# Attention inside a feed-forward kernel: plain heads' q and k change engines, steps of batches one to four change slots

## The chip, the core and the metric

The kernel runs on one core of a Trainium2 chip. The core has five engines with an instruction queue each: TensorE (PE, the matmuls), ScalarE (ACT), VectorE (DVE), GpSimd (POOL, which here issues the loads) and SyncE (SP, which here issues the stores and the DMA transposes). They run beside each other and wait for one another by semaphores. The metric is the device time of one execution in microseconds (us), the median of several runs.

## The reference

q, k and v have 8 batches, 8 heads, 576 tokens and 64 values a head. Heads 0 to 3 ("plain") let a token look at itself and the 31 tokens before it; heads 4 to 7 ("dilated") at every fourth token back to 128:

```python
mask_plain = (rel >= 0) & (rel < window)                                      # window = 32
mask_dil = (rel >= 0) & (rel < window * dilation) & (rel % dilation == 0)     # dilation = 4
scores = np.where(masks[None, :, :, :], scale * (q @ k^T), -1000000000.0)
attn = softmax(scores);  o = attn @ v
x = o.transpose(0, 2, 1, 3).reshape(8 * 576, 512)
h = np.maximum(x @ w_in, 0.0);  out = (h * h) @ w_out                         # w_in 512x2048, w_out 2048x512
```

(The two lines with `@` and `softmax` are shortened from the reference.) The 4608 rows of x go through the feed-forward layer (FFN) with a squared relu; the output is float32.

## The kernel before

**Storage.** On the chip everything is bf16, sums are float32 in PSUM. Heads go in pairs `e`: 0 and 1 are plain, 2 and 3 dilated. x is kept transposed in the ring `xT` (features on partitions, four batches of tokens), which the attention writes and the FFN reads.

**FFN.** Tokens go in four tiles of 256 and then tiles of 512. A tile is a list of *groups*: first-layer groups (`g1`, `mm1`, L660 to L682) are four matmuls of 512 columns (or eight of 256) into a bank of the pool `ps_f`, a relu on ACT into `h2T` (L681) and its square on DVE (L682). Second-layer groups (`g2`, L697 to L712) are four matmuls into another bank of `ps_f`; after the fourth of them ACT copies the bank to `osb` (L711) and SP stores it (L634). The last 128 tokens are done in two column halves of 256. In the kernel before both halves live in one bank. 512 tokens make 32 groups, all of them 288.

**Attention.** It is cut into steps, named by the batch, a letter and the head pair:

- `L` loads q and k (`q`) or v by POOL; `L..:x` is the DMA transpose of q and k on SP (`cross`, L213)
- `q`, `k`, `Q`, `K` (capitals: second part of the tokens): q or k is transposed and copied to `qT` or `kbd`. In batch 1, and for batch 2's plain heads, PE transposes into a bank of `ps_a` and the copies read PSUM (`trans`, L221 to L238); in the other cases the copies read what the DMA transposed (`xx`). Four copies to a step for the plain heads and for q (`halves`, L240 to L267)
- `v`, `V`: a dilated head's v is spread into `vbd` (two DVE copies, L207)
- `a`, `b`: scores of the first and second part: matmuls of `kbd` and `qT` into `ps_a`, an Exp on ACT, a mask product on DVE (L295 to L317)
- `o`, `p`: matmuls by v into `po` and sums into `pd` (L413, L415), Ln and Exp of the sums on ACT (L417, L418), and their product on DVE into `xT` (L428) (`pv`)

**Banks.** PSUM has `ps_f` with four banks, `ps_a` with two, and one each for `po` and `pd` (L111 to L114). A step that takes a bank waits until the bank's last reader is done. The odd pairs of batch 1 take two of `ps_f` for `po` and `pd` (L450 and L451).

**Which engine copies.** For plain heads q goes by ACT in batches 1 to 3 and by DVE from batch 4 (`ADDED = 4`), k always by DVE; dilated heads copy both on DVE (L225, L440).

**Order.** The order of all instructions is that of the program: the scheduler is manual, and each engine's queue follows it. The main loop (L836 to L848) emits one FFN group and after it the attention steps that the string `PROGRAM` (L21 to L36) has between its bars for this place. I call a group with the steps behind it a *slot*: slot n is group n (counted from 0 in the order in which the groups run) and then what stands behind bar n + 1. From batch 5 on most steps come from a formula with fixed offsets (L826 to L832), which isn't touched. The first field of `PROGRAM` is batch 0's attention in finer steps, run before any group.

Of the kernel before, what the change touches and what calls it, by code (L numbers as in the profile page):

```python
# [23 lines left out]
    "T20k C20v T30 C30v h W3 S20 E20 W2 S30 E30 T01 C01v T11 C11v W2 P00 P10 D00 D10 L00 X00 M00 B01 B11 P20 "  # L24
    "P30 D20 D30 L20 X20 M20 S01 T21 C21a T31 C31v E01 W2+11 S11 E11 | B21 S21 E21 | B31 S31 E31 P21 P31 D21 "
    "D31 L21 X21 M21 L31 X31 M31 | | P01 P11 D01 D11 L01 X01 M01 L11 X11 M11 | | | | | | | | | | | | | m n | | "
    "| | | L2:q00123 L2:q10123 | 1q1 1q3 | 1q2 1k2 | 1k1 1v3 | 1a2 | 1v2 1k0 1q0 | 1o2 | 1a0 1a1 | 1k3 1o0 1o1 "
    "| 1a3 1Q0 | 1K0 1o3 | 1Q1 1K1 | 1Q2 | 1b0 | | 1Q3 1K2 L2:vwpdr L3:q00123 L3:q10123 | L2:x | | 2q0 | | 2k0 "
    "1V2 | 1b2 1p0 | 1b1 1V3 1K3 | | 1p2 1p1 | 2a0 1b3 | 2k1 2o0 2b0 1p3 | 2q1 2k2 L3:x | | 2q2 2p0 L3:vwpdr "
    "2a1 | | | 2b1 | 2o1 2q3 2a2 | | 2p1 2v2 | 2k3 | 2b2 2o2 | 2v3 | 2a3 2p2 L4:q10123 | 2b3 3k1 | 2o3 3q1 | | "  # L30
    "3a1 L4:q00123 2p3 | 3k0 3k2 | | 3o1 | | | 3q0 3v2 | | | | 3a0 | 3b1 3k3 | | | 3p1 L4:x 3q2 L4:vwpdr | | "
    "3b0 | 3a2 3q3 3o0 4k0 | | | 3o2 3b2 | | 3p0 3v3 | 4q1 3a3 | 3p2 4q2 4q0 | L5:q10123 3b3 | 3o3 | 4k1 | | "
    "L5:q00123 3p3 4k2 4k3 4a0 L5:vwpdr | | | 4b0 | | 4q3 | | 4o0 | | | 4a2 4v2 | 4b2 | 4a3 L5:x 4a1 | 4o2 | | "
    "| 4p2 L6:q00123 4v3 | | 4b1 | | 4p0 | | 4p1 | 5q0 5k0 | 4b3 | | | | 4o1 | | 5k2 L6:q10123 4o3 | 5q2 5k1 | "
    "| 4p3 | 5q1 |"
)  # L36


# [25 lines left out]
def kernel(  # L64
# [9 lines left out]
    nc = tc.nc  # L74
    P = nc.NUM_PARTITIONS
    B, H, S, D = q.shape
    DM, DFF = moe_w_in.shape
    NTOK = B * S
# [7 lines left out]
    NE = H // 2  # L86
# [9 lines left out]
    PARTED = (0, 1)  # L96
    STAGE = (0, 1, 0, 2, 2, 2, 0, 1)
    ADDED = 4
# [51 lines left out]
    def staged(b: int, nm: str):  # L150


        t = rb[STAGE[b]][nm]
        return t[:, :].rearrange("p (a h x) -> p a h x", h=H, a=2)
# [47 lines left out]
    def spread_v(b: int, e: int, parts):  # L202

        p0, p1 = parts[0], parts[-1] + 1
        for hl in range(2):
            rows = slice(64 * hl, 64 * hl + 64)
            nc.vector.tensor_copy(  # L207
                vbd[b % 2][rows, e, RES * p0 : RES * p1, rows],
                vds[b][rows, e - NE // 2, p0:p1, :].rearrange("p m (r d) -> p (m r) d", d=D),
            )  # L210
# [7 lines left out]
            staged(b, nm)[0:n, part, h0:, :].rearrange("p h x -> p (h x)"),  # L218
        )

    def trans(b: int, e: int, nm: str, part: int):  # L221

        ps = ps_a.tile([P, 1024], bf16, name="pa")
        t = staged(b, nm)
        copy = nc.scalar.copy if nm == "q" and e < NE // 2 else nc.vector.tensor_copy  # L225
        if b == 2:
            m0, n, pitch, cuts = 0, M, M, [(t[0:80, a, :, :], MS[a], 80) for a in range(2)]
        else:

            m0, n, pitch, cuts = MS[part], MN[part], 80, [(t[0:80, part, :, :], 0, 80)]  # L230
        pv_ = ps[:, 0 : 4 * pitch].rearrange("p (h c m) -> p h c m", h=2, c=2)
        for hl in range(2):
            for c in range(2):
                for src, c0, w in cuts:
                    nc.tensor.transpose(  # L235
                        pv_[:, hl, c, c0 : c0 + w], src[:, 2 * e + hl, P * c : P * c + P], ident[0:w, 0:w]
                    )
        halves(e, nm, pv_[:, :, :, 0:n], m0, n, copy)  # L238
# [193 lines left out]
    def step(b: int, code: str):  # L432

        what, e = code[0], int(code[1])
        part = int(what in "QKVbp")
        if what in "qk" and (b > XB or b == XB and e >= NE // 2):
            t = (qx if what == "q" else kx)[b % 2]
            by_act = what == "q" and e < NE // 2 and b < ADDED  # L440
            halves(
                e, what, t[:, 2 * e : 2 * e + 2, :, :], 0, M, nc.scalar.copy if by_act else nc.vector.tensor_copy
            )
        elif what in "qQkK":
            trans(b, e, what.lower(), part)
        elif what in "vV":
            spread_v(b, e, [part] if b in PARTED else [0, 1])
        elif what in "ab":
            scores(b, e, part)
        elif b in PARTED and e % 2:  # L450
            pv(b, e, part, ps_f, "pf")  # L451
        else:
            pv(b, e, part)
# [180 lines left out]
    def store(osb, pos: int, c0: int = 0, c1: int = DM):  # L634

        x = 0
        while x < P:
            b, y = divmod(pos + x, S)
            part = int(y >= RES * MN[0]) if b in PARTED else 0
            w = MN[part] if b in PARTED else M  # L640
            r, m = divmod(y - RES * MS[part], w)
            n = min(P - x, w - m)
            row = b * S + RES * (MS[part] + m) + r
            nc.sync.dma_start(out[row : row + RES * (n - 1) + 1 : RES, c0:c1], osb[x : x + n, c0:c1])
            x += n

    def ffn_groups(tk0: int, nt: int):

        early = NT <= tk0 <= 2 * NT
        h2 = h2_pool.tile([P, NF, NT], bf16, name="h2T")
        per = NT // nt
        kts = (0, 2, 1, 3) if tk0 >= NT else (0, 1, 2, 3) if tk0 == 0 else (2, 3, 0, 1)
        cut = 3 if tk0 >= NT else 2
        cur, acc = {}, {}

        cuts = [(0, nt)] if tk0 // RING == (tk0 + nt - 1) // RING else [(0, -tk0 % RING), (-tk0 % RING, nt)]

        def mm1(u, ks):  # L660
            if u not in acc:
                acc[u] = ps_f.tile([P, NT], f32, name="pf")
            for x in range(per):
                f = per * u + x
                piece = max(y for y in range(len(w_in_sb)) if w_cuts[y] <= P * f)
                c0 = 512 * (f // 4) + f % 4 - w_cuts[piece]
                for kt in ks:
                    for y0, y1 in cuts:
                        t0 = (tk0 + y0) % RING
                        nc.tensor.matmul(  # L670
                            acc[u][:, nt * x + y0 : nt * x + y1],
                            w_in_sb[piece][:, kt, c0 : c0 + 509 : 4],
                            xT[:, kt, t0 : t0 + y1 - y0],
                            start=(kt == kts[0] and x == 0 and y0 == 0),
                            stop=(kt == kts[-1] and x == per - 1 and y1 == nt),
                            skip_group_check=True,
                        )
            if ks[-1] != kts[-1]:
                return
            hv = h2[:, per * u : per * u + per, 0:nt]  # L680
            nc.scalar.activation(hv, acc[u][:, :].rearrange("p (x n) -> p x n", x=per), ACT.Relu)  # L681
            nc.vector.tensor_tensor(out=hv, in0=hv, in1=hv, op=ALU.mult)  # L682

        def g1(i):
            if i < 2 and tk0 < NT:
                for u in range(2):
                    mm1(u, kts[2 * i : 2 * i + 2])
            elif i < 2 and early:
                for u in (2 * i, 2 * i + 1):
                    mm1(u, kts[:cut])  # L690
            elif i < 4 and early:
                for u in (2 * i - 4, 2 * i - 3):
                    mm1(u, kts[cut:])
            else:
                mm1(i, kts)

        def g2(m, part):  # L697
            if part == 0:
                cur[m] = ps_f.tile([P, DM], f32, name="pf")

            last = tk0 + P * (m + 1) == NTOK
            c0, c1 = (DM // 2 * (part // 2), DM // 2 * (part // 2 + 1)) if last else (0, DM)
            f0, f1 = (NF // 2 * (part % 2), NF // 2 * (part % 2 + 1)) if last else (4 * part, 4 * part + 4)
            for f in range(f0, f1):
                nc.tensor.matmul(  # L705
                    cur[m][:, c0:c1], h2[:, f, P * m : P * m + P], w_out_sb[:, f, c0:c1],
                    start=(f == 0), stop=(f == NF - 1),
                )
            if f1 == NF:
                osb = osb_pool.tile([P, DM], f32, name="osb")  # L710
                nc.scalar.copy(osb[:, c0:c1], cur[m][:, c0:c1])  # L711
                store(osb, tk0 + P * m, c0, c1)  # L712

        return [lambda i=i: g1(i) for i in range(NF // per)] + [
            lambda m=m, part=part: g2(m, part) for m in range(nt // P) for part in range(4)
        ]

# [161 lines left out]
```

## Time and profile before

| | |
|---|---|
| median of 6 runs | 314.06 us (312.62 to 315.2) |
| the profiled execution | 314.74 us, span from first to last instruction 313.0 us |
| granted TensorE clock | 0.993 |
| PE busy | 301.9 us, 96% |
| ACT busy | 197.5 us, 63%, 421 instructions |
| DVE busy | 195.6 us, 63%, 633 instructions |
| POOL busy | 94.0 us, 30% |
| DMA | 35.04 MB |

"Busy" is the time in which an engine has an instruction under way, as a share of the span. In the groups and in the timeline a row names the engine, the line of the kernel, the operation, `out<-in` by the program's names with partitions x elements, and how many instructions it counts. A bracket or the last column is the engine's idle time just before, and what ended it. Times in the timeline are from the span's start.

### The profile page before, as it was taken

To read this page: it belongs to the slowest core of one execution; us is meant where nothing else is said; L and a number is where in the kernel's file an instruction comes from. 1 tells how busy PE (TensorE), PEld (TensorE's weight loads), DVE (VectorE), ACT (ScalarE), POOL (GpSimd) and SP (SyncE) were. 2 spreads that over 40 slices of the span, in tenths; PEclk is the share of its full clock that TensorE was granted. 3 is DMA by queue.
4 is the path that set the end of the run, shared out by engine and by line. 5 is a ranking of instruction groups with operands and counts; after the bars stand their busy time and mean duration, and the time that the engine had idled before them with its cause. 6 is when DMAs were issued, how large, how long until landed. Compare 5 with 4: busy or idle time off the path is not lost.

```text
span 313.0 us, 6759 instructions
## 1 busy us (share of the span) xinstructions
PE 301.9 (96%) x2537; PEld 187.6 (60%) x2569; DVE 195.6 (63%) x633; ACT 197.5 (63%) x421; POOL 94.0 (30%) x138
## 2 busy tenths in 40 slices
PE   8899999999999999999999999999999999999994
PEld 3689745968755555565499655555555555445543
DVE  1336568898987878985799469946994334104400
ACT  7278838769878956785378547864686456226511
POOL 8679787626083127401451041000000000000000
PEclk9799999999999999999999999999999999999999
DMA  7999999999989899994699975602200210121022
GB/s 107 195 175 215 202 161 182 195 163 198 140 120 210 118 183 137 141 191 63 89 137 121 167 120 88 115 8 63 67 3 0 69 68 0 36 67 34 2 67 67
DMA packets 79808, 35.04 MB, mean 112 GB/s; under 512 B 49824, under 2 KB 74784, under 8 KB 79776
## 3 DMA queue, kind: packets, MB, share of 16 engines
q0 software_dynamic: 46592, 18.23, 51.6%
q1 hardware_dynamic: 32496, 16.06, 26.1%
q10 hardware_dynamic: 688, 0.33, 0.5%
q8 instruction: 20, 0.33, 0.5%
q14 instruction: 12, 0.10, 0.1%
HBM read 36.90 MB, written 9.44 MB: 148 GB/s over the span
## 4 chain that ended last, share of the span: by engine, by line
PE 84%; ACT 6%; DVE 2%; DMA 2%; issue 2%; POOL 1%; ACTq 0%; POOLq 0%
PE pf L670 37%; PE pf L705 36%; PE po L413 3%; PE pd L415 2%; DMA kb<-in_k_dram 2%; PE pa L304 2%; ACT h2T L681 2%; PE pa L310 1%; ACT qT L248 1%; PE pa L235 1%; ACT rec L417 1%; DVE kbd L252 1%; ACT rec L418 1%; ACT osb L711 1%; DVE xT L428 1%
## 5 line engine op out<-in xcount | busy, mean ns | idle before, releaser
L670 PE MATMUL pf<-xT,w_in 128*128 128x256 bf16 (+1 forms) x758 | 132.6, 325 | 1.1 <-DVE xT L428 0.3
L705 PE MATMUL pf<-w_out_sb,h2T 128*128 128x512 bf16 (+1 forms) x570 | 130.9, 373 | 1.7 <-ACT osb L711 0.5
L670 PEld LDWEIGHTS <-w_in 128*128 128x128 bf16 x768 | 82.3, 114 | 35.9 <-issue 1.2
L681 ACT ACTIVATE h2T<-pf 128x512 bf16<-128x512 f32 x144 | 83.7, 597 | 23.2 <-PE pf L670 22.5
L705 PEld LDWEIGHTS <-h2T 128*128 128x128 bf16 x592 | 54.3, 98 | 54.0 <-issue 0.7
L682 DVE TENSOR_TENSOR h2T<-h2T 128x512 bf16<-128x512 bf16 x144 | 58.0, 423 | 40.0 <-ACT h2T L681 38.4
L711 ACT COPY osb<-pf 128x512 f32<-128x512 f32 (+1 forms) x37 | 21.2, 573 | 42.2 <-PE pf L705 39.9
L428 DVE TENSOR_TENSOR xT<-po,rec 128x288 bf16<-128x288 f32 (+2 forms) x52 | 23.7, 456 | 31.1 <-ACT rec L418 30.4
L178 POOL DMA_DIRECT2D vbd<-in_v_dram x36 | 25.7, 730 | 55.5 <-PE pd L415 49.5
L417 ACT ACTIVATE rec<-pd 128x288 f32<-128x288 f32 (+2 forms) x52 | 21.5, 413 | 24.0 <-PE pd L415 22.9
L314 ACT ACTIVATE pt<-pa 128x352 bf16<-128x352 f32 (+6 forms) x56 | 27.6, 499 | 9.0 <-PE pa L310 4.7
L418 ACT ACTIVATE rec<-rec 128x288 f32<-128x288 f32 (+2 forms) x56 | 24.8, 444 | 1.8
L413 PEld LDWEIGHTS <-vbd 128*128 128x128 bf16 x286 | 16.8, 97 | 10.5 <-DVE vbd L207 1.2
L248 DVE COPY qT<-xx 64x288 bf16<-64x288 bf16 x80 | 20.0, 250 | 1.1
L161 POOL DMA_DIRECT2D qb<-in_q_dram x18 | 13.0, 722 | 22.2 <-DMA xx<-qb 20.8
L252 DVE COPY kbd<-xx 64x288 bf16<-64x288 bf16 x40 | 18.8, 470 | 0.6
L413 PE MATMUL po<-pt,vbd 128*128 128x96 bf16 (+3 forms) x263 | 18.0, 198 | 0.7 <-DVE vbd L207 0.5
L191 POOL DMA_DIRECT2D vd<-in_v_dram x24 | 14.7, 636 | 5.9 <-DMA kb<-in_k_dram 3.1
L415 PE MATMUL pd<-pt,mk 128*128 128x96 bf16 (+5 forms) x158 | 16.3, 203 | 0.0
L161 POOL DMA_DIRECT2D kb<-in_k_dram x18 | 12.8, 713 | 0.8 <-issue 0.8
L304 PE MATMUL pa<-qT,kbd 128*128 128x96 bf16 (+2 forms) x146 | 12.2, 201 | 0.5 <-ACT qT L248 0.5
L197 POOL DMA_DIRECT2D vbd<-in_v_dram x16 | 9.7, 615 | 9.2 <-PE pd L415 7.4
(89 smaller groups left out, 237.0 us busy)
## 6 DMA issues: line engine op xcount, KB each, us to landing
out_dram<-osb SPq DMA_DIRECT2D x18, 128.0 KB, 4.8
qb<-in_q_dram POOLq DMA_DIRECT2D x7, 320.0 KB, 7.5
kb<-in_k_dram POOLq DMA_DIRECT2D x7, 320.0 KB, 9.3
vd<-in_v_dram POOLq DMA_DIRECT2D x32, 64.0 KB, 4.8
w_in<-in_moe_w_in_dram POOLq DMA_DIRECT2D x4, 512.0 KB, 7.5
w_out_sb<-in_moe_w_out_dram POOLq DMA_DIRECT2D x4, 512.0 KB, 12.0
qb<-in_q_dram POOLq DMA_DIRECT2D x7, 256.0 KB, 5.9
kb<-in_k_dram POOLq DMA_DIRECT2D x7, 256.0 KB, 7.4
```

Of the source, the lines that this page charges most:

```text
L161: nc.gpsimd.dma_start(t[0:n, part, hs, :], src[b, hs, t0 : t0 + RES * n, :].rearrange("h (p r) d -> p h (r d)", r=RES))
L178: nc.gpsimd.dma_start(dst[rows, e, i0:i1, rows], v[b, 2 * e + hl, 64 * i0 : 64 * i1, :].rearrange("(i p) d -> p i d", p=64),)
L314: nc.scalar.activation(pt[:, off : off + n], ps[:, 0:n], ACT.Exp, scale=SCALE)
L413: nc.tensor.matmul(oo, vb[:, e, i, :], rh, start=(x == 0), stop=(x == len(mms) - 1), skip_group_check=True)
L417: nc.scalar.activation(rec[:, 0:n], d[:, 0:n], ACT.Ln)
L418: nc.scalar.activation(rec[:, 0:n], rec[:, 0:n], ACT.Exp, scale=-1.0)
L428: nc.vector.tensor_tensor(out=tok, in0=o if o is o3 else o[:, 0:n], in1=rec if o is o3 else rec[:, 0:n], op=ALU.mult)
L670: nc.tensor.matmul(acc[u][:, nt * x + y0 : nt * x + y1], w_in_sb[piece][:, kt, c0 : c0 + 509 : 4], xT[:, kt, t0 : t0 + y1 - y0], start=(kt ...
L681: nc.scalar.activation(hv, acc[u][:, :].rearrange("p (x n) -> p x n", x=per), ACT.Relu)
L682: nc.vector.tensor_tensor(out=hv, in0=hv, in1=hv, op=ALU.mult)
L705: nc.tensor.matmul(cur[m][:, c0:c1], h2[:, f, P * m : P * m + P], w_out_sb[:, f, c0:c1], start=(f == 0), stop=(f == NF - 1),)
L711: nc.scalar.copy(osb[:, c0:c1], cur[m][:, c0:c1])
```

## The change

It has four parts.

1. *Who copies.* A plain head's k is copied by ACT (batches 1 to 4), its q by DVE. A step whose code ends with `a` is copied by ACT whatever it is: `1q1a`, `1Q3a` and `2q3a`.
2. *Banks.* A step whose code ends with `f` takes `po` and `pd` from `ps_f`: `1o1f`, `1p1f`, `1p3f`, `2p1f`, `2p2f`. Before, it was `1o1`, `1o3`, `1p1`, `1p3`.
3. *The last tile* takes a second bank of `ps_f` for its second column half.
4. *Slots.* These differ (loads that stand beside unmoved steps are left out):

| slot | before | after |
|---|---|---|
| 21 | (loads of batch 2) | `1q1a 1q3`, then these loads |
| 22 | `1q1 1q3` | `1q2` |
| 23 | `1q2 1k2` | `1k2 1k1` |
| 24 | `1k1 1v3` | `1v3` |
| 40, 41 | –, `2k0 1V2` | `2k0`, `1V2` |
| 47 | `2k1 2o0 2b0 1p3` | `2o0 1p3f 2b0 2k1` |
| 54, 55, 56 | `2o1 2q3 2a2`, –, `2p1 2v2` | `2o1 2a2 2q3a`, `2v2`, `2p1f` |
| 61, 62, 63 | `2b3 3k1`, `2o3 3q1`, – | `2b3 2o3`, –, `2p3` |
| 64, 65 | `3a1` (a load) `2p3`, `3k0 3k2` | `3k1 3q1` (the load), – |
| 66, 67 | –, `3o1` | `3a1`, `3k0` |
| 68, 69 | –, – | `3o1`, `3k2` |

The other slots hold the same steps (with the suffixes above). In all ACT gets 440 instructions in place of 420, DVE 613 in place of 633; PE has the same number, and POOL and SP the same order.

```diff
--- before.py
+++ after.py
@@ -24,15 +24,15 @@
     "T20k C20v T30 C30v h W3 S20 E20 W2 S30 E30 T01 C01v T11 C11v W2 P00 P10 D00 D10 L00 X00 M00 B01 B11 P20 "
     "P30 D20 D30 L20 X20 M20 S01 T21 C21a T31 C31v E01 W2+11 S11 E11 | B21 S21 E21 | B31 S31 E31 P21 P31 D21 "
     "D31 L21 X21 M21 L31 X31 M31 | | P01 P11 D01 D11 L01 X01 M01 L11 X11 M11 | | | | | | | | | | | | | m n | | "
-    "| | | L2:q00123 L2:q10123 | 1q1 1q3 | 1q2 1k2 | 1k1 1v3 | 1a2 | 1v2 1k0 1q0 | 1o2 | 1a0 1a1 | 1k3 1o0 1o1 "
-    "| 1a3 1Q0 | 1K0 1o3 | 1Q1 1K1 | 1Q2 | 1b0 | | 1Q3 1K2 L2:vwpdr L3:q00123 L3:q10123 | L2:x | | 2q0 | | 2k0 "
-    "1V2 | 1b2 1p0 | 1b1 1V3 1K3 | | 1p2 1p1 | 2a0 1b3 | 2k1 2o0 2b0 1p3 | 2q1 2k2 L3:x | | 2q2 2p0 L3:vwpdr "
-    "2a1 | | | 2b1 | 2o1 2q3 2a2 | | 2p1 2v2 | 2k3 | 2b2 2o2 | 2v3 | 2a3 2p2 L4:q10123 | 2b3 3k1 | 2o3 3q1 | | "
-    "3a1 L4:q00123 2p3 | 3k0 3k2 | | 3o1 | | | 3q0 3v2 | | | | 3a0 | 3b1 3k3 | | | 3p1 L4:x 3q2 L4:vwpdr | | "
-    "3b0 | 3a2 3q3 3o0 4k0 | | | 3o2 3b2 | | 3p0 3v3 | 4q1 3a3 | 3p2 4q2 4q0 | L5:q10123 3b3 | 3o3 | 4k1 | | "
-    "L5:q00123 3p3 4k2 4k3 4a0 L5:vwpdr | | | 4b0 | | 4q3 | | 4o0 | | | 4a2 4v2 | 4b2 | 4a3 L5:x 4a1 | 4o2 | | "
-    "| 4p2 L6:q00123 4v3 | | 4b1 | | 4p0 | | 4p1 | 5q0 5k0 | 4b3 | | | | 4o1 | | 5k2 L6:q10123 4o3 | 5q2 5k1 | "
-    "| 4p3 | 5q1 |"
+    "| | | 1q1a 1q3 L2:q00123 L2:q10123 | 1q2 | 1k2 1k1 | 1v3 | 1a2 | 1v2 1k0 1q0 | 1o2 | 1a0 1a1 | 1k3 1o0 "
+    "1o1f | 1a3 1Q0 | 1K0 1o3 | 1Q1 1K1 | 1Q2 | 1b0 | | 1Q3a 1K2 L2:vwpdr L3:q00123 L3:q10123 | L2:x | | 2q0 | "
+    "2k0 | 1V2 | 1b2 1p0 | 1b1 1V3 1K3 | | 1p2 1p1f | 2a0 1b3 | 2o0 1p3f 2b0 2k1 | 2q1 2k2 L3:x | | 2q2 2p0 "
+    "L3:vwpdr 2a1 | | | 2b1 | 2o1 2a2 2q3a | 2v2 | 2p1f | 2k3 | 2b2 2o2 | 2v3 | 2a3 2p2f L4:q10123 | 2b3 2o3 | "
+    "| 2p3 | 3k1 3q1 L4:q00123 | | 3a1 | 3k0 | 3o1 | 3k2 | 3q0 3v2 | | | | 3a0 | 3b1 3k3 | | | 3p1 L4:x 3q2 "
+    "L4:vwpdr | | 3b0 | 3a2 3q3 3o0 4k0 | | | 3o2 3b2 | | 3p0 3v3 | 4q1 3a3 | 3p2 4q2 4q0 | L5:q10123 3b3 | "
+    "3o3 | 4k1 | | L5:q00123 3p3 4k2 4k3 4a0 L5:vwpdr | | | 4b0 | | 4q3 | | 4o0 | | | 4a2 4v2 | 4b2 | 4a3 L5:x "
+    "4a1 | 4o2 | | | 4p2 L6:q00123 4v3 | | 4b1 | | 4p0 | | 4p1 | 5q0 5k0 | 4b3 | | | | 4o1 | | 5k2 L6:q10123 "
+    "4o3 | 5q2 5k1 | | 4p3 | 5q1 |"
 )
 
 
@@ -218,11 +218,12 @@
             staged(b, nm)[0:n, part, h0:, :].rearrange("p h x -> p (h x)"),
         )
 
-    def trans(b: int, e: int, nm: str, part: int):
+    def trans(b: int, e: int, nm: str, part: int, home: str):
 
         ps = ps_a.tile([P, 1024], bf16, name="pa")
         t = staged(b, nm)
-        copy = nc.scalar.copy if nm == "q" and e < NE // 2 else nc.vector.tensor_copy
+        by_act = home == "a" or nm == "k" and e < NE // 2
+        copy = nc.scalar.copy if by_act else nc.vector.tensor_copy
         if b == 2:
             m0, n, pitch, cuts = 0, M, M, [(t[0:80, a, :, :], MS[a], 80) for a in range(2)]
         else:
@@ -433,21 +434,21 @@
 
 
 
-        what, e = code[0], int(code[1])
+        what, e, home = code[0], int(code[1]), code[2:]
         part = int(what in "QKVbp")
         if what in "qk" and (b > XB or b == XB and e >= NE // 2):
             t = (qx if what == "q" else kx)[b % 2]
-            by_act = what == "q" and e < NE // 2 and b < ADDED
+            by_act = home == "a" or what == "k" and e < NE // 2 and b <= ADDED
             halves(
                 e, what, t[:, 2 * e : 2 * e + 2, :, :], 0, M, nc.scalar.copy if by_act else nc.vector.tensor_copy
             )
         elif what in "qQkK":
-            trans(b, e, what.lower(), part)
+            trans(b, e, what.lower(), part, home)
         elif what in "vV":
             spread_v(b, e, [part] if b in PARTED else [0, 1])
         elif what in "ab":
             scores(b, e, part)
-        elif b in PARTED and e % 2:
+        elif home == "f":
             pv(b, e, part, ps_f, "pf")
         else:
             pv(b, e, part)
@@ -695,10 +696,10 @@
                 mm1(i, kts)
 
         def g2(m, part):
-            if part == 0:
+            last = tk0 + P * (m + 1) == NTOK
+            if part == 0 or last and part == 2:
                 cur[m] = ps_f.tile([P, DM], f32, name="pf")
 
-            last = tk0 + P * (m + 1) == NTOK
             c0, c1 = (DM // 2 * (part // 2), DM // 2 * (part // 2 + 1)) if last else (0, DM)
             f0, f1 = (NF // 2 * (part % 2), NF // 2 * (part % 2 + 1)) if last else (4 * part, 4 * part + 4)
             for f in range(f0, f1):
```

## The prediction

> **What bounds the kernel now.** I read the page's first two parts, the groups with shapes kept apart, the waits of TensorE (PE), and the timeline of 40 to 110 us and of the last 20 us, with the program's slots laid beside it.
>
> ```profile
> span 313.0 us, 6759 instructions
> PE 301.9 (96%) x2537; PEld 187.6 (60%) x2569; DVE 195.6 (63%) x633; ACT 197.5 (63%) x421; POOL 94.0 (30%) x138
> ```
>
> PE sets the end, and neither version has more matmuls than the other. So only PE's stalls can be won or lost. From 126 us on PE runs through: 27.77 us busy of the 28 from 132 to 160. The stalls lie in slots 21 to 66 (41 to 97 us), where the attention of batches 1 to 3 passes through ScalarE (ACT) and VectorE (DVE). The busy column hides part of them, since a matmul's row outlasts its streaming (379 ns in the row, 216 ns from start to start for 512 columns). I therefore took the distance between matmul starts less the streaming time, and left out gaps of 0.22 us, each one missing record.
>
> Stalls before, in us: 41 to 78 us: 0.32 (`1q2`), 0.39 (`1k1`), 0.25 (`1k0`), 0.51 (`1o2`), 0.17 (`1a0`), 0.42 (slot 32), 0.17 (`2q0`), 0.25 (slot 49), together 2.48. 78 to 92 us: 0.25 (`2p1`), 0.36 (`2o2`). 92 to 97 us: 0.62 (`3a1`), 0.43 (slot 66). Last tile: 0.5. All together 4.6 us: no change of order or banks can win more. The waits of PE name four of them:
>
> ```profile
> PE pf L705 <- ACT osb L711: 0.5, 1, 0.5
> PE pa L304 <- ACT qT L248: 0.5, 1, 0.5
> PE pf L670 <- DVE xT L428: 0.3, 1, 0.3
> PE pf L670 <- ACT osb L711: 0.3, 1, 0.3
> ```
>
> Prices of the swapped copies (count after x; then busy us, mean ns of one):
>
> ```profile
> L248 DVE COPY qT<-xx 64x288 bf16<-64x288 bf16 x80 | 20.0, 250 | 1.1
> L252 DVE COPY kbd<-xx 64x288 bf16<-64x288 bf16 x40 | 18.8, 470 | 0.6
> L248 ACT COPY qT<-xx 64x288 bf16<-64x288 bf16 x8 | 3.4, 427 | 0.1
> L248 ACT COPY qT<-pa 64x288 bf16<-64x288 bf16 x8 | 3.1, 392 | 0.3 <-PE pa L235 0.2
> ```
>
> [...] k writes every second element (470 ns). [...] slot 63's copy of the output ran only at 94.17, behind four q copies of 92.41 to 94.14, with its matmuls over at 92.3. [...]
>
> **The change, part by part.**
>
> *Who copies.* A plain head of batch 3 has 4x427 ns (q) on ACT and 4x470 (k) on DVE. After it, DVE has 4x250 = 1.0 us, and ACT has k at a price that no row shows. Below: 427 ns from SBUF[...]; above: 530[...]. I take 427 (392 from PSUM, 260 and 285 for the two parts of batch 1). DVE's q of 288 from PSUM has no row either: 222 ns for 128 and 238 for 160 give 305; the bounds 250 and 480. Batch 4's k leaves DVE for ACT (8x470 against 8x427); PE did not stall there, so it buys nothing, and slots 81 and 91 have an ACT that waits for PE. Two dilated q steps go to ACT, `1Q3a` and `2q3a`, 4 copies each; `1q1a`, a plain one, keeps its 4 there.
>
> *Slots 21 to 51.* I walked the three queues in program order with these durations, 0.2 us from a matmul's streaming end to its reader and 0.05 us back, as in the trace. Gone: the waits for `1v2`, for slot 31's copy (other bank) and for `1p3`'s product (its slot's order, and `2k1` off DVE). New: `1q2` 0.79 (ACT does the output copy of slot 21 until 41.61, then `1q1a` until 42.71; PE is there at 41.97), `1k1` 0.18, `1k3` and `1o0`/`1o1` 0.33, `1o3` and `1K1` 0.21, `1Q2` 0.62 (ACT: copy 0.59, `1K0` 1.18, `1o3` 0.82, `1K1` 1.18 in one row), `1b2` 0.10, `2o0` 0.24 and `1p3` 0.15 (now ahead of 0.6 us of PE work that covered their masks). Sum 2.62 against 2.48: **+0.15**.
>
> *Slots 52 to 63.* `2q3a` stands on ACT ahead of slot 55's relu:
>
> ```profile
> 83.56 0.59 ACT L681 ACTIVATE h2T<-pf 128x512 bf16<-128x512 f32 x1
> 83.63 0.95 DVE L248 COPY qT<-xx 64x288 bf16<-64x288 bf16 x4
> 84.91 0.42 DVE L682 TENSOR_TENSOR h2T<-h2T 128x512 bf16<-128x512 bf16 x1
> 85.80 0.60 DVE L207 COPY vbd<-vd 64x512 bf16<-64x512 bf16 x2
> 86.45 0.35 PE L413 MATMUL po<-pt,vbd 128*128 128x96 bf16 x5 [0.19 <-DVE vbd L207]
> ```
>
> The relu (83.56) moves 4x427 later and ends near 86.0. Behind it in DVE's queue stand its square (0.42), then `2v2` (0.60), for which `2o2` waits: 87.2 in place of 86.45. PE would be there at 85.95, so 1.25 replaces 0.25+0.36; `2p1` in the FFN's banks saves only what is then lost. `2o3`, one slot earlier, waits some 0.1 for its mask. **+0.75**.
>
> *Slots 63 to 75.* `2p3` ahead of slot 64 removes 0.43, and k on ACT beside q on DVE the 0.62 (both done as PE arrives, about 0.05 late). But `3k0` now stands on ACT right after slot 67's relus:
>
> ```profile
> 96.85 2.06 ACT L681 ACTIVATE h2T<-pf 128x512 bf16<-128x512 f32 x4 [0.96 <-PE pf L670]
> 98.78 0.41 ACT L417 ACTIVATE rec<-pd 128x256 f32<-128x256 f32 x1
> 99.55 1.56 ACT L681 ACTIVATE h2T<-pf 128x512 bf16<-128x512 f32 x3
> 100.98 1.75 ACT L248 COPY qT<-xx 64x288 bf16<-64x288 bf16 x4
> 103.66 0.32 PE L304 MATMUL pa<-qT,kbd 128*128 128x96 bf16 x4
> ```
>
> Count from the start T of slot 66's matmuls. ACT: relus T+0.5 to 1.5, `3a1`'s Exp to 1.9, relus to 2.9, `3k0` to 4.55, slot 68's relu 5.15, `3o1`'s Ln and Exp 5.9, slot 69's relu 6.4. PE: `3o1` waits for `3a1`'s mask (0.42), slot 73 for slot 69's relu (0.29). DVE has nothing to do from 3.4 to 5.2, then: square, `3o1`'s product, slot 69's square to 6.85, `3k2` 1.45, slot 70's square 0.42, `3q0` 1.0, to 9.7. `3a0` needs `3q0`, and PE reaches it at 8.2: 1.55. New 2.3 against 1.05: **+1.25**. The late DVE queue holds `3q2` back for `3a2` too: 0.5 against 0.17, **+0.35**.
>
> *The last tile.*
>
> ```profile
> 306.96 0.37 ACT L711 COPY osb<-pf 128x256 f32<-128x256 f32 x1 [1.16 <-PE pf L705]
> 307.39 1.91 PE L705 MATMUL pf<-w_out_sb,h2T 128*128 128x256 bf16 x16 [0.51 <-ACT osb L711]
> ```
>
> With a bank of its own the second half does not wait for the first half's copy: 0.51 idle and the drain of the last matmul, **-0.6**. Nothing covers it; bounds 0.4 and 0.65. Loads and stores keep their order on POOL and SP, and their issue is far from the path.
>
> Sum: 0.15+0.75+1.25+0.35-0.6 = +1.9: span 314.9, and the profiled execution 314.74+1.9 = 316.6. That execution was 0.7 above the median 314.06 of the six runs, so for a median I forecast 315.9.
>
> **Rivals.**
>
> *Faster: the queues have room.* The two long new stalls both hang on ACT's lag behind PE. If ACT is 1.5 us less behind at slot 67 than in my walk, `3q0` ends as PE arrives and both terms of batch 3 vanish; if `2v2` meets an earlier relu, 0.75 goes too. For it: in the timeline ACT waits 0.96 us for PE before 96.85, and DVE saves 0.9 us per head. Against: the FIFO order above. The removed 1.05 and the tail then count in full: -0.45 (1.05 less 0.6 still lost at `3o1` and slot 73), -0.6, and -0.9 in slots 21 to 63, together -2: 312.0. It decides where `3q0` ends before slot 74's matmuls do.
>
> *A wash.* One of the two long stalls comes, the other half or not at all: +1.9-1.5 = +0.4, 314.4, with 313.3 to 315.4.
>
> *k dear on ACT.* At 530 ns, each set of four adds 0.4 us; six sets stand ahead of a waiting PE (`1K0`, `1K1`, `2k0`, `2k1`, `3k1`, `3k0`), of which I let four count: +1.6, 317.5.
>
> **How the numbers follow.** Forecast 0.40 (its own range 315.2 to 316.9), dear k 0.13, wash 0.28, faster 0.19. The range that leaves out 2 in 10 runs from 311.8, just below the faster rival, to 318.0, just above the dear one. A measurement of this kernel can tell about 0.5%, 1.57 us: below 312.49 is faster, above 315.63 slower. Slower: 0.13 and most of 0.40, 0.51. Faster: most of the rival, 0.18. The rest, 0.31, is within.
>
> **What would show it.** Right: four kbd copies of about 427 ns on ACT between slot 67's and 68's relus, DVE idle before the square behind them, a PE wait for DVE's qT before `3a0` near 105 us, a wait for DVE's vbd of a microsecond before `2o2`, and no idle between the two halves of the last tile. Wrong: `3a0` and `2o2` start without a wait, or k copies on ACT of well over 430 ns; then the batch's terms change in size or sign.

## The result and the profile after

The changed kernel takes 316.97 us (median of 33 runs, 315.54 to 319.96), the kernel before 314.07 (70 runs). The ratio is 1.0099, with a 95% interval of 1.0082 to 1.0116: 3.1 us slower (2.6 to 3.6). The prediction said slower, 315.9, with 311.8 to 318.0 as its range. Of the executions whose granted clock is on record, those at 0.997 or more have medians of 316.1 us (22 of the changed kernel) and 313.5 us (112 of the kernel before), 2.6 us apart.

The page of the changed kernel, its first two lines:

```profile
span 314.9 us, 6761 instructions
PE 300.4 (95%) x2537; PEld 187.1 (59%) x2569; DVE 184.0 (58%) x613; ACT 206.9 (66%) x441; POOL 93.9 (30%) x138
```

DVE lost 11.6 us of work and ACT gained 9.4. PE's row is 1.5 us lower with the same matmuls, but not because of the change: in the first 16 us it is 1.7 lower (11.58 against 13.30, with a granted clock of 1.00 against 0.89). The loss is in where PE stands, and that is in its waits (engine, line, waited for: us in total, times, longest):

```profile
PE pa L305 <- DVE qT L249: 1.1, 1, 1.1
...
PE po L414 <- DVE vbd L207: 0.9, 1, 0.9
PE pa L236 <- ACT kbd L253: 0.5, 1, 0.5
PE pa L236 <- ACT qT L249: 0.5, 1, 0.5
PE pf L671 <- ACT h2T L682: 0.5, 2, 0.3
```

The four waits shown of before are all gone from the list: for `osb` (the last tile and slot 31's copy), for `qT` by ACT (`3a1`, of whose 0.62 us 0.23 is left) and for `xT` (`2p3`). In their place stand one for q (`3a0`), one for v (`2o2`), two in batch 1's copies, and a new kind: PE waits for a relu of the FFN itself. (The lines of the code have moved by one: L249 is the copy of q, L253 that of a plain k, L682 the relu, L683 the square.)

**The wait before `2o2`.** In the timeline of the changed kernel (start, duration, engine, line, operation; in brackets the idle time before and what ended it):

```profile
83.61 1.74 ACT L249 COPY qT<-xx 64x288 bf16<-64x288 bf16 x4
...
85.37 0.60 ACT L682 ACTIVATE h2T<-pf 128x512 bf16<-128x512 f32 x1
...
86.00 0.43 DVE L683 TENSOR_TENSOR h2T<-h2T 128x512 bf16<-128x512 bf16 x1 [1.89 <-ACT h2T L682]
...
86.34 0.60 DVE L207 COPY vbd<-vd 64x512 bf16<-64x512 bf16 x2
...
87.00 0.35 PE L414 MATMUL po<-pt,vbd 128*128 128x96 bf16 x5 [0.95 <-DVE vbd L207]
```

`2q3a` (83.61) stands ahead of slot 55's relu. DVE has nothing to do for 1.89 us because the square waits for that relu, and behind the square stand the copies of v that PE needs.

**The wait before `3a0`.** The same view, 15 us later:

```profile
98.84 2.09 ACT L253 COPY kbd<-xx 64x288 bf16<-64x288 bf16 x4
100.95 0.60 ACT L682 ACTIVATE h2T<-pf 128x512 bf16<-128x512 f32 x1
...
101.58 0.42 DVE L683 TENSOR_TENSOR h2T<-h2T 128x512 bf16<-128x512 bf16 x1 [2.31 <-ACT h2T L682]
101.60 1.02 PE L671 MATMUL pf<-xT,w_in 128*128 128x512 bf16 x4 [0.27 <-ACT h2T L682]
...
102.81 1.89 PE L671 MATMUL pf<-xT,w_in 128*128 128x512 bf16 x8 [0.18 <-ACT h2T L682]
...
104.80 0.95 DVE L249 COPY qT<-xx 64x288 bf16<-64x288 bf16 x4
...
105.81 0.32 PE L305 MATMUL pa<-qT,kbd 128*128 128x96 bf16 x4 [1.11 <-DVE qT L249]
```

`3k0` holds ACT for 2.09 us, DVE is idle for 2.31 and then does in a row what it could have done in them: `3k2`'s eight copies between 103.13 and 104.4, and `3q0` last. PE waits twice for a bank whose relu is late, and then for q.

**The last tile** runs through. No row of PE stands between ACT's two copies of 256 columns:

```profile
305.63 5.38 PE L706 MATMUL pf<-w_out_sb,h2T 128*128 128x512 bf16 x40
...
309.35 0.37 ACT L712 COPY osb<-pf 128x256 f32<-128x256 f32 x1 [1.16 <-PE pf L706]
311.09 0.37 ACT L712 COPY osb<-pf 128x256 f32<-128x256 f32 x1 [1.37 <-PE pf L706]
```

### The profile page after: what moved, and what is told of

It reads as the page before. It is cut to its first block, busy times and chain, and to the rows that moved or that the text cites. A ratio compares the mean times of both kernels' runs of the same rounds, so it can differ in the third digit from the quotient of the medians.

```text
span 314.9 us, 6761 instructions
## 1 busy us (share of the span) xinstructions
PE 300.4 (95%) x2537; PEld 187.1 (59%) x2569; DVE 184.0 (58%) x613; ACT 206.9 (66%) x441; POOL 93.9 (30%) x138
## 4 chain that ended last, share of the span: by engine, by line
PE 80%; ACT 7%; DVE 5%; DMA 3%; issue 2%; POOL 2%; ACTq 0%; POOLq 0%
PE pf L706 36%; PE pf L671 33%; PE po L414 3%; DMA vd<-in_v_dram 3%; ACT h2T L682 3%; PE pd L416 2%; PE pa L305 2%; ACT kbd L253 1%; PE pa L311 1%; DVE qT L249 1%; DVE h2T L683 1%; DVE kbd L260 1%; PE pa L236 1%; POOL qb L161 1%; ACT qT L249 1%
## 5 line engine op out<-in xcount | busy, mean ns | idle before, releaser
L682 ACT ACTIVATE h2T<-pf 128x512 bf16<-128x512 f32 x144 | 83.7, 597 | 22.3 <-PE pf L671 21.6
L683 DVE TENSOR_TENSOR h2T<-h2T 128x512 bf16<-128x512 bf16 x144 | 58.1, 423 | 44.2 <-ACT h2T L682 42.8
L249 DVE COPY qT<-xx 64x288 bf16<-64x288 bf16 x84 | 21.2, 252 | 1.2
L414 PE MATMUL po<-pt,vbd 128*128 128x32 bf16 (+3 forms) x256 | 17.5, 198 | 1.4 <-DVE vbd L207 0.9
L416 PE MATMUL pd<-pt,mk 128*128 128x32 bf16 (+6 forms) x150 | 15.9, 204 | 0.0
L305 PEld LDWEIGHTS <-kbd 128*128 128x128 bf16 x146 | 9.0, 97 | 4.8 <-issue 1.4
```

Source lines behind the costliest of these rows:

```text
L249: copy(qT[rows, e, :, m0 : m0 + n].rearrange("p (c j) m -> p j c m", j=2)[:, jj, :, :], src)
L305: nc.tensor.matmul(ps[:, n : n + w].rearrange("p (r m) -> p r m", r=RES), kbd[:, e, i, :], qT[:, e, :, m0:m1], start=True, stop=True,)
L414: nc.tensor.matmul(oo, vb[:, e, i, :], rh, start=(x == 0), stop=(x == len(mms) - 1), skip_group_check=True)
```

## The experiments

Each was timed beside the kernel before. The start of the kernel, where loads set the pace (the chain that leads to the first FFN matmul stands for 7.27 us on one landing of a load in before, for 8.23 in the changed kernel), varies: the first FFN matmul came at 16.3 to 19.0 us in the thirteen traces. So I compare traces by **the stretch** from the first FFN matmul to the last matmul of the kernel, and ratios by the timed runs.

| kernel | ratio to before (95%) | stretch, us |
|---|---|---|
| before | 1 | 291.42 |
| before, again (`e11_before_again`) | 1.0001 (0.9975–1.0026) | 290.89 |
| changed | 1.0099 (1.0082–1.0116) | 293.16 |
| changed, again (`e10_after_again`) | 1.0094 (1.0057–1.0132) | 293.23 |
| `e1_tail` | 0.9964 (0.9943–0.9986) | 290.43 |
| `e2_q0_first` | 1.0059 (1.0038–1.0080) | 292.55 |
| `e3_q3_later` | 1.0040 (1.0022–1.0059) | 292.22 |
| `e4_swap` | 1.0139 (1.0112–1.0166) | 296.08 |
| `e5_k0_dve` | 1.0007 (0.9982–1.0032) | 290.86 |
| `e6_joined` | 0.9943 (0.9920–0.9965) | 289.21 |
| `e7_no_swap` | 0.9980 (0.9960–1.0001) | 289.50 |
| `e8_k_in_line` | 1.0089 (1.0052–1.0126) | 293.04 |
| `e9_k_packed` | 1.0063 (1.0033–1.0092) | 292.77 |

The theory under test is the prediction's: the loss comes from two places where a set of copies on ACT stands ahead of a relu (`2q3a`, `3k0`) and so starves DVE. Its rivals: the dear k copies (510 ns, where the prediction took 427), or the exchange of engines as such, wherever it stands.

**The last tile alone.** The kernel before with the second bank (the line that sets `last` moves up with it):

```diff
-            if part == 0:
+            if part == 0 or last and part == 2:
                 cur[m] = ps_f.tile([P, DM], f32, name="pf")
```

> The kernel before with one edit: the second bank for the last tile's second column half. Theory (the last tile's 0.51 us wait and the drain are bare): 0.6 us less than before, ratio 0.998, no gap between the halves in the trace. Rival (the end is set by the store behind the last copy, which both halves' stores share): no difference, ratio 1.000, with the gap gone all the same.

Measured: 313.65 us beside 314.17. The gap of 0.67 us between the starts of the halves, less the streaming, is gone. The ratio says 1.1 us, with an interval from 0.4 to 1.8 that includes the 0.6 expected. The rival, that the stores set the end, fell.

**`3q0` ahead of `3k2`.** The changed kernel with the two exchanged in slots 69 and 70:

```diff
-... | 3o1 | 3k2 | 3q0 3v2 | ...
+... | 3o1 | 3q0 | 3k2 3v2 | ...
```

> The changed kernel with 3q0 and 3k2 exchanged (slot 69: 3q0, slot 70: 3k2 3v2). Theory (3a0 waits because 3q0 stands behind 3k2's 1.9 us in VectorE's queue): the 1.27 us wait before 3a0 goes to under 0.2, 1.2 us less than the changed kernel, about 315.8, ratio to before 1.006. Rival (the dear k copies on ScalarE keep the relus late, so that PE waits there in any case): the wait is replaced by one for a relu or for 3k0, less than 0.4 us is won, ratio 1.009.

Measured: 316.43 us, ratio 1.0059. The wait before `3a0` is gone, so it was VectorE's order there. But half of it returned one stage on. `3p1` now waits 0.55 us (from start to start, less the streaming) for `3b1`'s mask:

```profile
108.67 0.40 DVE L316 TENSOR_TENSOR pt<-pt,mask_p 128x480 bf16<-128x480 bf16 x1
...
109.12 0.38 PE L414 MATMUL po<-pt,vbd 128*128 128x32 bf16 x6 [0.39 <-DVE pt L316]
```

The mask stands behind `3k2`, `3v2` and the squares. The stretch is 0.6 us shorter than the changed kernel's, about half of the 1.2 expected: the order moved the wait, but DVE's 2.3 us of lost time were still lost.

**`2q3a` two slots later**, behind `2p1f`:

```diff
-... | 2o1 2a2 2q3a | 2v2 | 2p1f | ...
+... | 2o1 2a2 | 2v2 | 2p1f 2q3a | ...
```

> The changed kernel with 2q3a moved from slot 54 to slot 56, behind 2p1f. Theory (2o2's wait of 1.12 us comes from 2q3a's four copies ahead of slot 55's relu on ScalarE): the wait falls to 0.4 or less, 0.7 us less than the changed kernel, about 316.2, ratio 1.007. Rival (2v2 is late because of VectorE's own load): the wait stays above 0.9, or it moves to 2a3, ratio 1.009.

Measured: 315.37 us, ratio 1.0040; the stretch is 0.94 us shorter than the changed kernel's. In its timeline slot 55's relu no longer waits for the copies, the square and `2v2` follow at once, and PE goes from `2b2` to `2o2` without a bracket:

```profile
82.92 0.59 ACT L682 ACTIVATE h2T<-pf 128x512 bf16<-128x512 f32 x1
...
83.54 0.43 DVE L683 TENSOR_TENSOR h2T<-h2T 128x512 bf16<-128x512 bf16 x1
83.88 0.60 DVE L207 COPY vbd<-vd 64x512 bf16<-64x512 bf16 x2
...
84.36 1.75 ACT L249 COPY qT<-xx 64x288 bf16<-64x288 bf16 x4
...
85.20 0.34 PE L414 MATMUL po<-pt,vbd 128*128 128x96 bf16 x5
```

The theory's first place is shown: the same four copies, two slots later, cost nothing.

**`3k0` back on VectorE, `3q0` back on ScalarE**, each in its new slot. With a suffix `v` that asks for DVE (and the same condition in `trans`):

```diff
-by_act = home == "a" or what == "k" and e < NE // 2 and b <= ADDED
+by_act = home == "a" or home != "v" and what == "k" and e < NE // 2 and b <= ADDED
-... | 3a1 | 3k0 | 3o1 | 3k2 | 3q0 3v2 | ...
+... | 3a1 | 3k0v | 3o1 | 3k2 | 3q0a 3v2 | ...
```

> The changed kernel with 3k0 copied by VectorE and 3q0 by ScalarE, as before the change, each in its new slot. Theory (3k0's four copies on ScalarE between the relus of slots 67 and 68 make slots 70 to 74 late): the waits of 0.44, 0.35 and 1.3 us go, those of 0.23 and 0.36 before them stay, 2.0 us less than the changed kernel, ratio to before 1.0035. Rival (VectorE has no room for 3k0's 1.9 us, so that 3o1's product, 3k2 and 3k3 pile up there): less than 0.7 us won, ratio 1.008 or more.

Measured: 314.11 us, ratio 1.0007; the stretch is 2.3 us shorter than the changed kernel's. Its timeline:

```profile
99.20 5.35 PE L671 MATMUL pf<-xT,w_in 128*128 128x512 bf16 x24
...
99.82 1.93 DVE L253 COPY kbd<-xx 64x288 bf16<-64x288 bf16 x4
...
101.63 1.74 ACT L249 COPY qT<-xx 64x288 bf16<-64x288 bf16 x4
...
104.39 0.32 PE L305 MATMUL pa<-qT,kbd 128*128 128x96 bf16 x4
```

PE runs 24 matmuls in a row where the changed kernel shows two waits for a relu, and `3a0` starts without one. DVE fills with k the very time in which it was idle. That `3k0` on ACT made the relus late is shown, and this second place is the larger: with this pair of moves alone nearly the whole loss is gone. `3a0`'s wait would not have gone with `3k0` alone: DVE was done with `3k2` at 104.16 and with slot 70's square at 104.62, so that a `3q0` of 1.0 us behind them on DVE would have ended near 105.6 (an estimate from these durations), 1.2 us after `3a0`'s start here. The two moves were not tried apart.

**The exchange alone, and all but the exchange.** First the kernel before with nothing but other engines for plain q and k:

```diff
-copy = nc.scalar.copy if nm == "q" and e < NE // 2 else nc.vector.tensor_copy
+copy = nc.scalar.copy if nm == "k" and e < NE // 2 else nc.vector.tensor_copy
-by_act = what == "q" and e < NE // 2 and b < ADDED
+by_act = what == "k" and e < NE // 2 and b <= ADDED
```

> The kernel before with the copies' engines exchanged for plain heads (k on ScalarE, q on VectorE), in its own slots and with its own banks. Theory (the loss is one of slots and queues, the dear copies of 510 ns add some): 0.3 to 0.8 us more than before, ratio 1.001 to 1.003. Rival (the exchange itself is the loss, six steps of 4 x 83 ns more ahead of a waiting PE): 2 us more, ratio 1.006 or over.

Measured: 318.89 us, ratio 1.0139: 4.4 us. I had expected a quarter of this at most, and the rival, the exchange itself, came in at twice its size. In the old slots the exchange is worse than the whole change. The longest wait, in its timeline:

```profile
93.68 2.08 ACT L252 COPY kbd<-xx 64x288 bf16<-64x288 bf16 x4
...
95.79 0.41 ACT L417 ACTIVATE rec<-pd 128x288 f32<-128x288 f32 x1
...
96.71 0.46 DVE L428 TENSOR_TENSOR xT<-po,rec 128x288 bf16<-128x288 f32 x1 [2.55 <-ACT rec L418]
97.08 1.00 DVE L248 COPY qT<-xx 64x288 bf16<-64x288 bf16 x4
98.14 0.32 PE L304 MATMUL pa<-qT,kbd 128*128 128x96 bf16 x4 [1.47 <-DVE qT L248]
```

It is the theory's mechanism in a third place: `3k1` on ACT (93.68) holds up `2o3`'s Ln, DVE is idle 2.55 us for the product behind it, and `3q1` stands behind the product. Before, the two copies ran side by side on two engines; now one waits for the other. This wait is 1.6 us from start to start, less the streaming. More than half of the loss (3.0 of 5.2 us in the stretch, against the second trace of before) comes earlier, in slots 21 to 51, with waits of 0.9 us before `1k2`, 0.7 before `1b2` and 1.4 in slot 49, which were not followed up. Then the other way round, the changed kernel's slots, banks and last tile with the old engines (plain q with `a` in batches 1 to 3, plain k with `v`, `1Q3` and `2q3` without a suffix):

> The changed kernel's slots, banks and last tile, with the copies on the engines of the kernel before (plain q of batches 1 to 3 on ScalarE, all else on VectorE). If the exchange is the whole loss whatever the slots: 1.0099 less 0.0139, ratio 0.996, 1.2 us less than before. If slots and engines depend on each other (the new slots are bad for the old engines, as the old slots were for the new ones): 1.000 or more.

Measured: 312.90 us, ratio 0.9980, just short of a clear gain. So, in ratios: the exchange costs 1.4% in the old slots and 1.2% in the new ones (where it has `1Q3a` and `2q3a` in it, which the run before this one left on DVE); slots, banks and last tile together win 0.2% with the old engines and 0.4% with the new. The exchange is the loss and the rest is a small gain; in the stretch, against the second trace of before, the last tile is 0.67 us of its 1.39. The banks were not tried alone.

The two like ratios hide a shift. In the old slots the exchange costs 3.0 us in slots 21 to 51 and 2.2 in slots 52 to 75; in the new ones it costs 0.5 and 2.8 to 3.1 (against the second trace of before in the old slots, against this run in the new). So the new slots took most of its price out of batches 1 and 2, and what they left stands in the slots of the theory's two places.

**What makes k dear on ScalarE.** In the changed kernel's groups (mean ns of one is the number behind the comma):

```profile
L253 ACT COPY kbd<-xx 64x288 bf16<-64x288 bf16 x16 | 8.2, 510 | 0.2
L253 ACT COPY kbd<-pa 64x288 bf16<-64x288 bf16 x8 | 3.8, 479 | 0.5 <-PE pa L236 0.5
```

k's source is read in turns from two rows of 144 elements, and its target is every second element. First the source was read as it lies (this kernel and the next leave out the order in which k's elements have to stand):

```diff
-src.rearrange("p c (i m) -> p i m c", m=16)
+src.rearrange("p c m -> p (c m)").rearrange("p (i x) -> p i x", x=32)
```

> The changed kernel, but the plain heads' k copies of 288 elements read their source in the order in which it lies (batches 2 to 4; k then stands in a wrong order, the instructions and elements are as many). If the alternating source makes them dear on ScalarE, 510 ns become some 427, and of the loss go 0.3 us at 3k0 and up to 0.3 each at 2k0, 2k1 and 3k1: 0.5 to 1.0 us, ratio 1.007. If the target's stride of two elements makes them dear: 510 ns and ratio 1.010 stay.

```profile
L257 ACT COPY kbd<-xx 64x288 bf16<-64x288 bf16 x16 | 8.1, 509 | 0.2
```

Nothing changed. The expectation's first half fell. Then the target was packed too:

```diff
-kbd[rows, e, :, rows].rearrange("p i (x j) -> p j i x", j=2)
+kbd[rows, e, :, rows].rearrange("p i (j x) -> p j i x", j=2)
```

> As the run that reads k in line, and the copies of 288 elements also write runs of 32 elements side by side in place of every second element (batches 2 to 4; k then stands in a wrong order). If the target's stride makes k dear on ScalarE, 510 ns become some 427 (480 some 392 from PSUM), and the waits behind 3k0 shrink by 0.3 us each: 0.44 and 0.35 to about 0.1, 1.27 to about 0.95, together some 1 us less than the changed kernel, ratio 1.007. If something else does, 510 ns and the waits stay.

```profile
L257 DVE COPY kbd<-xx 64x288 bf16<-64x288 bf16 x24 | 7.1, 296 | 0.3
L257 ACT COPY kbd<-xx 64x288 bf16<-64x288 bf16 x16 | 6.8, 427 | 0.2
L257 ACT COPY kbd<-pa 64x288 bf16<-64x288 bf16 x8 | 3.1, 391 | 0.5 <-PE pa L236 0.5
```

It is the target's step of two elements (a packed target with the alternating source was not tried). What the dearness cost is less clear. The first wait for a relu behind `3k0` (0.44 us), that before `3a1` (0.23) and one before `3p0` (0.2) went; the second for a relu (0.35) and `3a0`'s (1.27) stayed; and `2o2`'s grew from 1.12 to 1.39 us, as `2v2`'s copies took 0.88 us in place of 0.60 beside a load issue of GpSimd (see the last section). The stretch is 0.4 us shorter than the changed kernel's and the ratio 0.36% lower, with intervals that overlap. The dear k is a part of the loss, and not its main one.

**Both kernels once more**, for second traces:

> The changed kernel once more, unaltered, for a second trace. The traces of the two kernels differ by 1.74 us from the first FFN matmul to the last matmul, the timed runs by 3.1. If the changed kernel's profiled execution was a lucky one in slots 21 to 75, this one shows waits that the first lacks, of 0.5 to 1.2 us; if the rest lies before the first FFN matmul (16.5 to 19.0 us in the traces so far) or behind the last, the stretch takes 293.2 us again.

> The kernel before once more, unaltered, for a second trace. Its ratio to itself should be 1.000. If its first trace was an unlucky one, the stretch from the first FFN matmul to the last takes some 0.4 us less than 291.4 (the waits for 1k1 and 1o2 are then 0.18 and 0.31 us, as in the run with the last tile's banks alone); else 291.4 again.

The changed kernel repeats to 0.07 us in the stretch, with its long waits alike (1.12 us before `2o2`, 1.27 before `3a0`); some 0.2 us of short waits moved from slots 76 to 89 into slots 52 to 75. The kernel before does not repeat so well: its first trace had 0.39 and 0.51 us before `1k1` and `1o2`, the second 0.18 and under 0.12. Against the second trace the change adds 2.3 us to the stretch rather than 1.7. What may have made the first longer is in the last section.

**A version that beats both**: the kernel before up to slot 53; behind it the changed kernel's slots and banks, with `2q3a` in slot 56, `3k0v` and `3q0a`, and the exchange for `3k1` and `3q1` alone; the last tile with two banks.

> A version meant to beat both: slots, engines and banks of the kernel before up to slot 53; from there the changed kernel's slots and banks with 2q3a in slot 56, k on ScalarE and q on VectorE for 3k1 and 3q1 alone; two banks in the last tile. Theory: the waits for 2p1, 2o2, 3a1 and 2p3 and the last tile's go (0.25, 0.36, 0.62, 0.43, 0.6), some 0.5 us comes for 3a1 and 3o1: 1.7 us less than before, ratio 0.9945. Rival (batch 3's copies pile up on VectorE as in the changed kernel): no better than the last tile's two banks alone, ratio 0.9965 or more.

Measured: 312.18 us beside 313.87, ratio 0.9943, 1.8 us less than before; the stretch is 289.21, 1.2 us shorter than with the last tile's banks alone (the intervals of the two ratios overlap). PE has no gap above 0.2 us left between 78 and 94 us, two in batch 3 (0.23 before `3a1`, 0.36 before `3o1`, both in the changed kernel too), and up to 78 us those of before.

## Why the prediction was right

The prediction gave slower a chance of 0.51, little better than even. The two long waits came where its walk of the queues had put them; the timed loss of 3.1 us is larger than its sum of 1.9, and the median lies 0.07 us above the forecast's own range of 315.2 to 316.9. Its steps against the two pairs of traces: I take the distance of FFN groups from the first FFN matmul, since a group's start has the waits of all slots ahead of it:

| step | predicted | first pair | second pair |
|---|---|---|---|
| slots 21 to 51 | +0.15 | +0.06 | +0.56 |
| slots 52 to 75 (`2q3a`, batch 3) | +2.00 | +2.10 | +2.46 |
| slots 76 to 89 (`3q2` for `3a2`) | +0.35 | +0.23 | -0.04 |
| last tile | -0.60 | -0.65 | -0.64 |
| sum | +1.90 | +1.74 | +2.34 |

*Who copies.* This step failed in its price. k on ScalarE was bounded by 427 and 530 ns and taken at 427; it measured 510, near the upper end (a price of well over 430 ns was one of the prediction's own signs of being wrong), and 333 and 298 for batch 1's parts in place of 285 and 260. The 427 was ACT's row for q, carried over to k as if length alone set the price. That was my assumption: ACT's copies of the masks from SBUF do follow their length in before (401 ns for 128x256, 423 for 128x288, 453 for 128x320), and so did k with the packed target (427 and 391 ns), but not this one, so the measurement decides. The 530 was an assumption too, drawn from no row; the alternating source is not what brings the price near it, since with that source taken away the copy took 509 ns. The other new row, DVE's q from PSUM, was put at 305 ns (the two rows that it was drawn from give 302) and measured 306. Batch 4's k was said to buy nothing; it cost 0.1 to 0.2 us. `4k0`'s 2.06 us on ACT stand ahead of what `3p0` needs, and `3p0` waits for that long in the seven traces with this dear `4k0` on ACT, and in none of the six where DVE copies it or k is packed.

*Slots 21 to 51.* Near wait by wait: `1q2` 0.65 us for 0.79, `1k1` 0.18 for 0.18, `1Q2` 0.67 for 0.62, `1o3` and `1K1` 0.28 for 0.21, `2o0` 0.28 for 0.24, `1p3` 0.13 for 0.15; `1k3`, `1o0` and `1o1` took 0.14 for 0.33, and `1b2`'s 0.10 did not come. What was off is the kernel before: 0.7 of the 2.48 us that the change was to win there were waits of one execution.

*`2q3a`.* The relu was to end near 86.0 and `2o2` to start at 87.2; they did at 85.97 and 87.00. `e3_q3_later` confirms the cause.

*Batch 3.* `3a0`'s wait is 1.27 for 1.55, `3o1`'s 0.36 for 0.42, slot 73's 0.35 for 0.29. A wait for slot 68's relu of 0.44 had not been seen, and `3a1`'s was 0.23 for 0.05; these are what the dear k adds, since they go when k takes 427 ns. That ACT works through its queue in order is what the step rests on; the traces show it (in the changed kernel the relu at 100.95 starts right behind `3k0`'s copies of 98.84 to 100.93, though the last row of its matmuls had ended at 99.60), and taking `3k0` out of ACT's queue, with `3q0` into it later, removed all of these but `3o1`'s and `3a1`'s.

*`3q2` late for `3a2`* failed: 0.18 us as before, not 0.5 (and under 0.1 in the second trace). The table's +0.23 is the 0.2 us before `3p0`; in the second pair the 0.24 us that before has at `3a2` is gone and offsets it. PE's own wait before `3a0` had let DVE catch up; that is my reading, and `e2_q0_first` fits it, since without that wait PE stands for DVE again further on.

*The rivals.* The faster one needed ACT to be 1.5 us less behind at slot 67, and the wash needed one of the two long waits to fail; both waits came, with 1.27 us of 1.55 and 1.12 of 1.25. The rival of the dear k was near in its price and wrong in its size: it asked for 1.6 us, and the packed k gave back 0.4 in the trace. The median of 316.97 lies nearer to its 317.5 than to the forecast's 315.9, but not for its reason.

*What the sum leaves.* The timed runs say 3.1 us (2.6 to 3.6), the second pair 2.3 in the stretch. From the last matmul's start to the end the changed kernel took 4.1 us in both traces, the kernel before 3.9: 0.2 more, all of it after the last store had landed. Together that is the 2.6 us of the executions with a granted clock of 0.997 or more. The other 0.5 us seems to lie ahead of the first FFN matmul. In eight of the thirteen traces the granted clock was 0.59 to 0.84 between 8 and 16 us, and the first FFN matmul came at 17.6 to 19.0 us; in the other five the clock was 1.00 there and it came at 16.3 to 17.6. Of the executions on record, half of the changed kernel's (22 of 44) had a mean granted clock below 0.997, and a third (57 of 169) of the kernel before's. Whether the change has a part in that is not shown. That the profiled span came out at the predicted 314.9 is partly luck: in the first pair the first FFN matmul came at 17.58 and 17.60 us, though the start varies by 2.7 us, and the 0.2 us at the end, which the sum lacks, made up for what it had too much in the stretch (1.90 for 1.74).

## What to carry to other kernels

Which engine has fewer busy microseconds says little about where a copy may stand: between two relus of a stage that feeds the other engine, 2.09 us of copies on ScalarE left VectorE idle for 2.31 us here, and it paid them back ahead of what TensorE needed next, which then waited 1.27 us. So walk each queue, with the waits between the queues, from the moved step to the next step that TensorE waits for. And see two traces of the kernel before, or more, before the waits of one are counted as winnings.

## What was not expected of the hardware

- ScalarE's copy of 64x288 bf16 from SBUF takes 427 ns into a packed target and 510 into every second element; from PSUM 391 and 479. VectorE's takes 296 and 470. The order in which the source is read made no difference on ScalarE (510 and 509 ns into every second element).
- Some of DVE's copies took longer while GpSimd issued loads. Over the thirteen traces, the q copies of 64x288 from SBUF took 229 ns (711 of them, none over 233) with no load issue of GpSimd under way. Where an issue covered more than half of one (341 of them), most still took 232 or less, but 144 took over 263, up to 543. For a dilated head's v (64x512) it was 284 ns (at most 293) without an issue; of 63 under one, 24 took over 327, up to 570. The plain k copies of 64x288 into every second element (means of 469 without and 471 ns with one), q copies from PSUM (305 and 305) and the squares (423 and 425) did not care. The step of the target is not what decides: a dilated k's copies of 64x32, also into every second element, took 177 ns without and 281 on average with one, up to 499. Only some of VectorE's operations were touched; what sets them apart no run shows. My walk had left this out. It fits the spread of the kernel before, whose first trace has `1v2` beside two such issues (start, duration; GpSimd's rows are POOL):

```profile
46.69 0.72 POOL L161 DMA_DIRECT2D qb<-in_q_dram  x1
46.70 0.75 DVE L207 COPY vbd<-vd 64x256 bf16<-64x256 bf16 x2
47.64 0.68 POOL L161 DMA_DIRECT2D kb<-in_k_dram  x1 [0.23 <-issue]
47.67 0.67 DVE L207 COPY vbd<-vd 64x256 bf16<-64x256 bf16 x2
...
48.40 0.29 PE L413 MATMUL po<-pt,vbd 128*128 128x64 bf16 x4 [0.35 <-DVE vbd L207]
```

and whose second trace has the same four copies earlier, the first two beside an issue that did not slow them, and no wait:

```profile
46.02 0.46 DVE L207 COPY vbd<-vd 64x256 bf16<-64x256 bf16 x2
...
46.07 0.60 POOL L197 DMA_DIRECT2D vbd<-in_v_dram  x1 [0.84 <-DMA kb<-in_k_dram]
...
46.70 0.45 DVE L207 COPY vbd<-vd 64x256 bf16<-64x256 bf16 x2
...
47.21 0.29 PE L413 MATMUL po<-pt,vbd 128*128 128x64 bf16 x4
```

No run moved a load to test it; it is read from the traces alone, of before and of `e9_k_packed`.
